# Ten DMA transposes in place of identity products for q and k of the fourth batch

## The chip, the cores and the metric

The kernel runs on one core of one Trainium2 chip. The metric is the device time of one execution in microseconds (us). Three runs of the kernel before are known, and one further execution was recorded by the hardware profiler; every view quoted below comes from that one.

A core has four engines that compute: TensorE (PE in the views; PEld is its weight load), VectorE (DVE), ScalarE (ACT) and GpSimd (POOL). SyncE (SP) only issues DMAs here. DMAs are issued by POOL and by SP, and are carried out by 16 DMA engines.

## The reference

There are B = 8 batches, H = 8 heads, S = 576 tokens, D = 64 elements per head, and 16 extra "beacon" keys and values per head. First comes attention, then a mixer over its output:

```python
scores = scale * q @ concat(beacon_k, k).T        # 576 x 592 per head, causal but for the beacons
a = softmax(scores)
x = a @ concat(beacon_v, v)                       # heads side by side: 576 x 512 per batch
h = x.T @ U @ V                                   # rank 32, along the tokens
u = x + h.T
out = u + relu(u @ w_ch1) @ w_ch2                 # 512 -> 2048 -> 512
```

Inputs and output are float32. The kernel computes in float16, with float32 sums.

## The kernel before

**Counting.** Batches are b = 0 to 7, so the fourth batch is b = 3. Two heads make a pair c = 0 to 3, and p = 4b + c counts all pairs.

**Loads and staging.** For the batches 0 to 3, q and k are loaded in float16 by `token_load` (L224) from POOL: partition p holds the six tokens 6p to 6p+5 of each head, so a descriptor reads 6 x 64 float32 in one piece (1536 bytes). `emit_loads` (L259) issues for one batch the beacon keys, two halves of k and two of q, and then v (`v_beacon`, and five `v_tokens`, L239). For the batches 4 to 7, `load_whole` (L844) loads q and k in "token order": tile j holds 128 consecutive tokens, one token per partition, so a descriptor reads 64 float32 (256 bytes). These loads go into a list `coming`, from which one is issued with each unit of the mixer that `fill` emits. Both forms go into staging tiles (`st0` for k and `st1` for q), of which there are two buffers each, in `qk_tiles`.

**Turning q and k.** The scores need q and k with the head elements on partitions (`qT`, `kT`). For the batches 0 to 3, `regroup` (L290, L292) copies a pair's columns together on DVE. Then `qkT_units` multiplies six pieces of 96 tokens by an identity on PE into one PSUM bank (`in_pair`, L297), and DVE copies the bank into `qT` or `kT` (L330; the beacons' 16 columns at L335). For the batches 4 to 7, `turns` (L861) makes ten DMA transposes on SP instead: k tile 0, the five tiles of q, then k tiles 1 to 4, each for all heads (L869). `kT` has two buffers, for even and odd batches, and `qT` two.

**Scores and values.** `visit` makes scores (L409) for one or more groups of a pair and lets ACT take their exponential (L418). Masks follow on DVE (L346, L348), and `av_unit` multiplies by v (L427) and divides by the sums on DVE (L435, L436) into `xb`.

**The mixer.** When a batch is done, `mix_units` runs. `turn` (L455) sends five DMA transposes `uT<-xb` from SP. `head` (L464) and `most` (L489) compute the rank 32 part on PE in four PSUM banks. `settle` (L476) adds these banks on DVE to what the transposes put into `uT`, and `end` (L502) does the last 80 tokens. The blocks of 512 rows of the mixer then run as units out of `queue`, one with each `fill(1)`. The blocks 0 and 1 are `mlp_units` (L751, L777, with DVE or ACT taking out each bank), the later ones `fast_units` (L607, L633). A block's input is turned back by DMA transposes `ut<-uT` (L745, L583) for the last sum, and results are stored from SP (L796, L658).

**What sets the order.** The whole stream is in `tc.manual_schedule`: each engine and each queue does its work in the order in which the program names it. The order around the change is written out by hand. The loop over p starts at p = 8. At p = 8 it calls `load_batch(3)`, and then plays the line `third[0]`; the pairs 8 to 11 are `third`, and from p = 12 (`P6`) on `long_slot` is used. The products that turn batch 3 stand as q12, k12, q13, k13 in `third`, and for the pairs 14 and 15 in `long_slot` at p = 12 and 13. First scores of batch 3 are `v11:23,12:0` in `third[3]`; the next are `v12:123`. At p = 12 the program names on SP, in this order: k tile 0 and q tiles 0 to 3 of batch 4 (`fill_turns(tr, NT)`), `uT<-xb` of batch 2 (`mix_between`), and the other five transposes of batch 4. `most` of batch 2 is in `long_slot` at p = 13.

**Limits on the queues.** POOL's DMAs use eight completion semaphores in turn, and so do SP's: a DMA waits until the one eight places before it on its own queue has landed.

**PSUM banks.** `pst` (L106) takes the bank that has been empty longest, in program order (`emptied.pop(0)`), and `emptying` puts a bank at the end of that list. A PE instruction that starts a bank waits for the engine that last read it.

Of the kernel before, what the change touches and what calls it, by code (L numbers as in the profile page):

```python
# [30 lines left out]
def kernel(  # L31
# [13 lines left out]
    nc = tc.nc  # L45
# [13 lines left out]
    nk = [min(P, SK - P * c) for c in range(NC)]  # L59

    q0 = [max(0, P * j - Nb) for j in range(NC)]
    nq = [min(S, P * (j + 1) - Nb) - q0[j] for j in range(NC)]
    NT = NC
# [113 lines left out]
    kTs = [const.tile([P, NH2, NC * P], F16, name=f"kT{i}", tag=f"kT{i}") for i in range(2)]  # L177
    vss = [const.tile([P, NC * H * E], F16, name=f"vs{i}", tag=f"vs{i}") for i in range(2)]
# [41 lines left out]
    def beacon_load(eng, src, dst, hs):  # L220
        eng.dma_start(out=dst[0:Nb], in_=src[hs].rearrange("h p d -> p h d"))

    def token_load(eng, src, dst, hs):
        eng.dma_start(out=dst[0:TP, hs, :], in_=src[hs].rearrange("h (p j) d -> p h (j d)", j=TJ))  # L224

    def key_beacons(eng, src, dst, hs):
        beacon_load(eng, src, dst[TP:TB, hs, (TJ - 1) * D : TJ * D], hs)
# [15 lines left out]
    def v_loads(src, bsrc, vs):  # L243
        v_beacon(bsrc, vs)
        v_tokens(src, vs, ALLH)
# [4 lines left out]
    ALLH = slice(0, H)  # L250
# [5 lines left out]
        whole = [x[:, 0 : NT * DM].rearrange("p (j h d) -> p j h d", h=H, d=D) for x in t]  # L256
        return st, whole

    def emit_loads(b, L, vs):  # L259
        key_beacons(nc.gpsimd, beacon_k[b], L[0][0], ALLH)  # L260
        for hs in HALVES:
            token_load(nc.gpsimd, k[b], L[0][0], hs)
            token_load(nc.gpsimd, q[b], L[0][1], hs)
        v_loads(v[b], beacon_v[b], vs)


    def keep_warm(ps, n, a=ident):
# [15 lines left out]
    def regroup(st, c, i, *copies, beacons=True):  # L283

        t = pairs.tile([P, TJ, 2, D], F16, name=f"pr{i}", tag=f"pr{i}")
        src = by_token(st[i][:, 2 * c : 2 * c + 2, :])
        w = TJ // len(copies)
        for a, copy in enumerate(copies):
            js = slice(w * a, w * (a + 1))
            copy(out=t[0:TP, js], in_=src[0:TP, js])  # L290
        if i == 0 and beacons:
            copies[0](out=t[TP:TB, TJ - 1], in_=src[TP:TB, TJ - 1])  # L292
        return t
# [539 lines left out]
    Ls, qTs, xbs = {}, {}, {}  # L833
    coming = []

    def load_batch(b):
        if b < DT0:
            Ls[b] = qk_tiles()
            emit_loads(b, Ls[b], vss[b % 2])
        else:  # L840
            coming.append(lambda: v_beacon(beacon_v[b], vss[b % 2]))
            coming.extend(lambda j=j: v_tokens(v[b], vss[b % 2], ALLH, [j]) for j in range(NT))
# [15 lines left out]
        while coming:  # L858
            coming.pop(0)()

    def turns(b):  # L861

        all_coming()
        new_qT(b)
        kn, qn = Ls[b][1]
        k_of = lambda j: (kn, kTs[b % 2], P * j, nk[j], j)
        q_of = lambda j: (qn, qTs[b], q0[j], nq[j], j)
        return [
            lambda n=n, dst=dst, o=o, m=m, j=j: nc.sync.dma_start_transpose(  # L869
                out=dst[:, :, ds(o, m)], in_=n[:m, j, :, :].rearrange("p h d -> p (h d)")  # L870
            )
            for n, dst, o, m, j in [k_of(0), *map(q_of, range(NT)), *map(k_of, range(1, NT))]
        ]

    HALVES = [slice(0, H // 2), slice(H // 2, H)]
# [19 lines left out]
    prs = {}  # L895
    V = nc.vector.tensor_copy

    def regroup_of(p):
        b, c = divmod(p, NH2)
        prs[p] = [regroup(Ls[b][0], c, i, nc.vector.tensor_copy) for i in range(2)]  # L900

    for i in range(2):
        nc.vector.memset(kTs[i][:, :, SK : NC * P], 0.0)
# [15 lines left out]
    def qkT_of(p):  # L919
        b, c = divmod(p, NH2)  # L920
        new_qT_of(p)
        copies = [(act_copy, nc.vector.tensor_copy) if p == 0 else (nc.vector.tensor_copy,)] * 2
        turns = by_heads(Ls[b][0], c)
        for i, t in enumerate(prs.get(p, ())):
            if t is not None:
                turns[i] = in_pair(prs[p])[i]
        return qkT_units(turns, qTs[b], kTs[b % 2], c, copies, Ls[0][0][0] if p == 0 else None)

    def expts_of(p):
        return [(lent if p in (2, 3) else expts)[(2 * p + i) % NE] for i in range(2)]  # L930
# [21 lines left out]
    ON_PE = (0, 1, 4)  # L952

    DT0 = 4
    LAG = 10
    HINT = 5
    FAST = 2
# [10 lines left out]
    def fill_turns(tr, n):  # L968
        for u in tr[:n]:
            u()  # L970
        del tr[:n]
# [64 lines left out]
    with tc.manual_schedule(engines={ENG.PE, ENG.Activation, ENG.DVE, ENG.SP, ENG.Pool}):  # L1036
# [182 lines left out]
        for p in range(NP1, NP):  # L1219
            b, c = divmod(p, NH2)  # L1220
            if c == (1 if b >= DT0 else 0) and b + 1 < B:
                load_batch(b + 1)
            if c == (1 if b + 1 == DT0 else 2) and DT0 <= b + 2 < B:
                load_whole(b + 2)
            qk = qkT_of(p + 2) if P6 <= p and p + 2 < min(NP, DT0 * NH2) else []
            if c == 0 and DT0 <= b + 1 < B and b != DT0:
                tr = turns(b + 1)
            if c == NH2 - 1 and b + 1 == DT0:
                tr = turns(b + 2)
            if c in (0, NH2 - 1) and b + 1 == DT0:  # L1230
                fill_turns(tr, NT)
            if p == P6:
                mix_between(b - 1)
            if c == 0 and b + 1 >= DT0:
                fill_turns(tr, 2 * NT)
            if p < P6:
                play(third[c])
            else:
                long_slot(p, c, av_of(p), qk or [lambda: None] * 2)
# [110 lines left out]
```

## Time and profile before

| | |
|---|---|
| three runs | 341.88, 343.14, 347.04 us (median 343.14) |
| the profiled execution | 340.93 us, of which the span from first to last instruction is 339.3 |
| granted TensorE clock | 1.00 |
| busy DVE, ACT, POOL (share of the span) | 69%, 53%, 40% |
| mean rate of the DMAs | 124 GB/s |

How to read the rows of the next part: in a timeline a row has start, length, engine, line, operation, out<-in, a count if several neighbours were put together, and in square brackets the idle time before it and what ended that. In a chain a row has start, length and what. "SPq" is SP's queue issuing a DMA. In DMA views, q0 is the queue that POOL feeds, and q1 the one that SP feeds; a queue's row has packets, MB, and the time that its packets took as a share of 16 engines' window. A row under "issues" ends with the median time from issue to landing.

### The profile page before, as it was taken

The page shows a single profiled execution, that of the slowest core. Times are in us where ns is not written, and L with a number is a line of the kernel's source. Part 1 is how long each engine was busy: PE and PEld are TensorE (multiplying, and loading weights), DVE is VectorE, ACT ScalarE, POOL GpSimd, SP SyncE. Part 2 cuts the span into 40 slices and gives each one's busy share as a digit, 9 for nine tenths or more (in the row PEclk, how much of TensorE's full clock was granted, in tenths as well). Part 3 has the DMA queues.
Part 4 walks back from the last instruction along what each step waited for, and adds up shares of the span by engine and source line. Part 5 has one row for each costly group of instructions (what it writes and reads, how often), then busy time and mean ns, then how long its engine had stood idle before and what let it go on. Part 6 is the DMA issues. An engine that isn't in the chain of part 4 may idle for free.

```text
span 339.3 us, 8838 instructions
## 1 busy us (share of the span) xinstructions
PE 329.8 (97%) x3494; PEld 212.0 (62%) x3494; DVE 234.1 (69%) x585; ACT 178.7 (53%) x383; POOL 136.1 (40%) x175
## 2 busy tenths in 40 slices
PE   8799999999999999999999999999999999999993
PEld 4465655455555456865688888755875675585493
DVE  6586885689989748765876677687776963743652
ACT  5957951478851677257734784468445403502500
POOL 8986724765140900677066805040130014013041
PEclk9999999999999999999999999999999999999999
DMA  8999999999997994999999999944213304104113
GB/s 159 141 175 138 183 196 194 200 192 139 138 118 152 153 141 86 101 169 157 151 112 155 187 143 104 132 140 87 66 64 93 73 31 126 31 33 124 31 37 99
DMA packets 150832, 41.97 MB, mean 124 GB/s; under 512 B 132096, under 2 KB 149696, under 8 KB 150784
## 3 DMA queue, kind: packets, MB, share of 16 engines
q0 software_dynamic: 87568, 18.18, 74.6%
q1 hardware_dynamic: 62992, 22.87, 37.4%
q8 instruction: 29, 0.48, 0.6%
q10 hardware_dynamic: 224, 0.30, 0.3%
q14 instruction: 19, 0.16, 0.2%
HBM read 37.45 MB, written 9.44 MB: 138 GB/s over the span
## 4 chain that ended last, share of the span: by engine, by line
PE 88%; DMA 4%; POOL 3%; DVE 1%; issue 1%; ACT 1%; POOLq 0%; DVEq 0%
PE gps L607 29%; PE po L427 9%; PE mpsD L633 7%; PE cps L777 7%; PE gps L751 7%; PE sps L409 5%; DMA vs<-in_v_dram 4%; PE mpsF L633 4%; PE mpsC L633 4%; PE mpsA L633 4%; PE mpsB L633 4%; PE mpsE L633 3%; POOL vs L239 1%; PE sps L370 1%; POOL st L224 1%
## 5 line engine op out<-in xcount | busy, mean ns | idle before, releaser
L418 ACT ACTIVATE expt<-sps 128x496 f16<-128x496 f32 (+2 forms) x192 | 82.0, 539 | 52.6 <-PE sps L409 52.6
L607 PE MATMUL gps<-uT,w 128*128 128x512 f16 (+1 forms) x512 | 103.7, 353 | 0.0
L654 POOL TENSOR_TENSOR ob<-ob,ut 128x512 f32<-128x512 f32 x26 | 30.8, 1188 | 139.9 <-DVE ob L654 127.7
L633 PEld LDWEIGHTS <-gT 128*128 128x128 f16 x800 | 75.1, 98 | 11.3 <-issue 2.1
L618 ACT ACTIVATE gT<-gps 128x512 f16<-128x512 f32 x84 | 49.7, 609 | 58.8 <-PE gps L607 54.3
L607 PEld LDWEIGHTS <-w 128*128 128x128 f16 x512 | 47.6, 98 | 41.4 <-issue 1.6
L239 POOL DMA_DIRECT2D vs<-in_v_dram x50 | 39.7, 804 | 15.3 <-DMA w<-in_moe_w_ch_dram 12.3
L596 DVE TENSOR_TENSOR gT<-gT 128x1024 f16<-128x1024 f16 (+2 forms) x77 | 39.5, 540 | 4.2 <-ACT gT L618 3.3
L427 PEld LDWEIGHTS <-expt 128*128 128x128 f16 x900 | 33.9, 98 | 10.9 <-issue 2.7
L427 PE MATMUL po<-vs,expt 128*128 128x65 f16 x900 | 36.5, 194 | 1.1 <-DMA vs<-in_v_dram 1.0
L616 DVE TENSOR_SCALAR gT<-gps 128x512 f16<-128x512 f32 x28 | 19.3, 691 | 24.0 <-PE gps L607 23.4
L436 DVE TENSOR_TENSOR xb<-po,rec 128x320 f16<-128x320 f32 x64 | 31.4, 491 | 2.2
L751 PE MATMUL gps<-uT,w 128*128 128x512 f16 x128 | 32.5, 379 | 0.1
L777 PE MATMUL cps<-w,gT 128*128 128x512 f16 x128 | 31.1, 379 | 0.0
L435 DVE RECIPROCAL rec<-po 128x5 f32<-128x5 f32 x64 | 12.1, 189 | 19.0 <-PE po L427 18.7
L346 DVE TENSOR_TENSOR expt<-expt,bigmask 128x512 f16<-128x512 f16 x54 | 22.5, 417 | 1.2 <-ACT expt L418 1.2
L409 PE MATMUL sps<-qT,kT 64*128 64x80 f16 (+4 forms) x288 | 22.6, 281 | 0.0
L376 ACT ACTIVATE expt<-sps 128x496 f16<-128x496 f32 (+2 forms) x48 | 20.4, 564 | 0.6 <-PE sps L370 0.6
L409 PEld LDWEIGHTS <-kT 64*128 64x128 f16 x288 | 10.2, 94 | 13.4 <-issue 9.3
L777 PEld LDWEIGHTS <-gT 128*128 128x128 f16 x128 | 11.2, 98 | 11.6 <-issue 1.3
L852 POOL DMA_DIRECT2D st<-in_q_dram x20 | 16.9, 874 | 3.2 <-DVE expt L348 1.4
L751 PEld LDWEIGHTS <-w 128*128 128x128 f16 x128 | 10.6, 97 | 10.8 <-issue 1.2
(125 smaller groups left out, 384.8 us busy)
## 6 DMA issues: line engine op xcount, KB each, us to landing
out_dram<-ob SPq DMA_DIRECT2D x55, 128.0 KB, 1.9
vs<-in_v_dram POOLq DMA_DIRECT2D x18, 128.0 KB, 7.9
w<-in_moe_w_ch_dram POOLq DMA_DIRECT2D x4, 512.0 KB, 6.4
w<-in_moe_w_ch_dram POOLq DMA_DIRECT2D x2, 1024.0 KB, 12.8
out_dram<-ob SPq DMA_DIRECT2D x8, 256.0 KB, 4.9
st<-in_k_dram POOLq DMA_DIRECT2D x12, 128.0 KB, 7.2
st<-in_q_dram POOLq DMA_DIRECT2D x12, 128.0 KB, 8.3
st<-in_k_dram POOLq DMA_DIRECT2D x4, 288.0 KB, 11.9
```

Of the source, the lines that this page charges most:

```text
L239: nc.gpsimd.dma_start(out=dst[a : a + nq[j], j, :, :], in_=src[hs, ds(q0[j], nq[j]), :].rearrange("h p d -> p h d"))
L409: nc.tensor.matmul(banks[i][:, ds(at0 + o, w)], kT[hp, c, ds(P * ch, P)], qT[hp, c, ds(qa, w)], start=True, stop=True, skip_group_check=le ...
L418: nc.scalar.activation(out=at[p][3][i][:, ds(SLOT * g, gw[g])], in_=bank[:, ds(at0, gw[g])], func=AF.Exp, scale=scale)
L427: nc.tensor.matmul(po[:, j, :], ex[0 : nk[c], ds(blk[(c, j)], P)], vs[0 : nk[c], ds(c * H * E + h * E, E)], start=(c == 0), stop=(c == j),)
L436: nc.vector.tensor_tensor(out=xb[:, :, ds(h * D, D)], in0=po[:, :, 0:D], in1=r.broadcast_to([P, NT, D]), op=ALU.mult)
L596: nc.vector.tensor_tensor(out=o[:, ds(d0, n)], in0=x[:, ds(d0, n)], in1=y[:, ds(d0, n)], op=op)
L607: nc.tensor.matmul(g[:, ds(o, w)], w1[:, cc, ts(dc, P)], uT[:, cc, ds(at, w)], start=(cc == 0 and o == 0), stop=(cc == NCC - 1), skip_grou ...
L618: nc.scalar.activation(out=cell["g"][:, dc, :], in_=g, func=AF.Relu)
L633: nc.tensor.matmul(ps, a()[:, d, ds(P * i, P)], bm[:, d, ds(c0, w)], start=fresh and d == 0 and (i == 0 or key != bank), stop=d == HF - 1, ...
L654: eng.tensor_tensor(out=out, in0=x, in1=y, op=ALU.add)
L751: nc.tensor.matmul(g[:, 0:n], w1[:, cc, ts(dc, P)], uT[:, cc, ds(r0, n)], start=(cc == 0), stop=(cc == NCC - 1))
L777: nc.tensor.matmul(ps[:m, :], gT["t"][:, dc, ds(P * i, m)], w2[:, dc, :], start=(dc == 0), stop=turned and dc == NDC - 1, skip_group_check ...
```

## The change

Batch 3 is loaded in token order by POOL like the batches 4 to 7, but at one place in `emit_loads`, not through `coming`: the beacon keys, k tile 0, the five tiles of q, k tiles 1 to 4, then v. Right after these loads, still at p = 8 and ahead of `third[0]`, SP is given the ten transposes of batch 3. The regroups of the pairs 12 to 15, their identity products and their copies are gone; their places in the hand-written order stay, empty.

```diff
-    def emit_loads(b, L, vs):
-        key_beacons(nc.gpsimd, beacon_k[b], L[0][0], ALLH)
+    def emit_loads(b, L, vs, whole=""):
+        if "k" not in whole:
+            key_beacons(nc.gpsimd, beacon_k[b], L[0][0], ALLH)
         for hs in HALVES:
-            token_load(nc.gpsimd, k[b], L[0][0], hs)
-            token_load(nc.gpsimd, q[b], L[0][1], hs)
+            for i, (name, src) in enumerate((("k", k[b]), ("q", q[b]))):
+                if name not in whole:
+                    token_load(nc.gpsimd, src, L[0][i], hs)
+        if whole:
+            for u in whole_loads(b, L, whole):
+                u()
         v_loads(v[b], beacon_v[b], vs)

+    def whole_loads(b, L, names):
+        def part(i, j):
+            src, m = ((k[b], nk), (q[b], nq))[i]
+            nc.gpsimd.dma_start(
+                out=L[1][i][m[j] - nq[j] : m[j], j, :, :],
+                in_=src[:, ds(q0[j], nq[j]), :].rearrange("h p d -> p h d"),
+            )
+        units = []
+        if "k" in names:
+            units += [lambda: beacon_load(nc.gpsimd, beacon_k[b], L[1][0][:, 0, :, :], ALLH)]
+        units += [lambda n=n, j=j: part("kq".index(n), j) for n, j in order_of(names)]
+        return units
+
+    def order_of(names):
+        return [x for x in [("k", 0)] + [("q", j) for j in range(NT)] + [("k", j) for j in range(1, NT)] if x[0] in names]
...
-            emit_loads(b, Ls[b], vss[b % 2])
+            emit_loads(b, Ls[b], vss[b % 2], AHEAD if b == DT0 - 1 else "")
...
-    def turns(b):
+    def turns(b, names="kq"):
...
-            for n, dst, o, m, j in [k_of(0), *map(q_of, range(NT)), *map(k_of, range(1, NT))]
+            for n, dst, o, m, j in [(k_of if x == "k" else q_of)(i) for x, i in order_of(names)]
...
-        prs[p] = [regroup(Ls[b][0], c, i, nc.vector.tensor_copy) for i in range(2)]
+        prs[p] = [
+            None if b == DT0 - 1 and name in AHEAD else regroup(Ls[b][0], c, i, nc.vector.tensor_copy)
+            for i, name in enumerate("kq")
+        ]
...
-        return qkT_units(turns, qTs[b], kTs[b % 2], c, copies, Ls[0][0][0] if p == 0 else None)
+        units = qkT_units(turns, qTs[b], kTs[b % 2], c, copies, Ls[0][0][0] if p == 0 else None)
+        return [
+            (lambda: None) if b == DT0 - 1 and name in AHEAD else u for name, u in zip("qk", units)
+        ]
...
     DT0 = 4
+    AHEAD = "kq"
...
                 load_batch(b + 1)
+                if b + 1 == DT0 - 1:
+                    fill_turns(turns(b + 1, AHEAD), 2 * NT)
```

## The prediction

> **What bounds the kernel now.** I read the page's first and fourth parts, PE's waits, and then the chain around the place of the change.
>
> ```profile
> span 339.3 us, 8838 instructions
> PE 329.8 (97%) x3494; PEld 212.0 (62%) x3494; DVE 234.1 (69%) x585; ACT 178.7 (53%) x383; POOL 136.1 (40%) x175
> PE 88%; DMA 4%; POOL 3%; DVE 1%; issue 1%; ACT 1%; POOLq 0%; DVEq 0%
> ```
>
> PE is busy 97% of the span and holds 88% of the chain. So only two things move the time: PE work that goes, and new waits of PE. The wait list around the change has one entry of some size:
>
> ```profile
> PE tps L297 <- DVE gT L766: 0.5, 1, 0.5
> ```
>
> The chain there, with the products that turn batch 3:
>
> ```profile
> 75.49 0.68 DVE pr L292
> ...
> 76.56 0.61 DVE gT L766
> ...
> 81.93 0.26 PE tps L297 x6
> ...
> 106.28 0.27 PE tps L297 x6
> ```
>
> The reader is to see that the first row belongs to the regroup of pair 12, that an eviction is queued behind it (second row), for which PE then waits 0.5 us, and that batch 3's eight groups of six products (first and last shown) take 0.26 to 0.27 us each of the chain.
>
> Now the DMAs, which PE does not wait for today. Two windows show them at work, the first with POOL's loads alone, the second with four transposes `ut<-uT` among them:
>
> ```profile
> q0 software_dynamic: 4669, 0.59, 246.8%
> ...
> q1 hardware_dynamic: 16, 0.00, 0.5%
> ```
>
> ```profile
> GB/s 150 138 176 182 218 225 294 301 208 163 149 161 259 172 163 172 114 54 29 42 47 19 9 82 158 159 157 164 169 166 160 168 146 156 158 188 154 149 152 158
> DMA packets 5651, 1.22 MB, mean 152 GB/s; under 512 B 5523, under 2 KB 5523, under 8 KB 5650
> q0 software_dynamic: 3392, 0.42, 131.5%
> q1 hardware_dynamic: 2258, 0.78, 76.2%
> ```
>
> The first is 84 to 88 us: 4669 small packets in 4.0 us, 1167 per us. The second is 74 to 82 us: in twice the time POOL's queue gets only 3392 packets through. Transposes are dear to the loads beside them; that decides the forecast.
>
> **The change part by part.**
>
> *PE.* Eight groups go: 8 x 0.265 = 2.1 us. The wait of 0.5 us goes with the regroup in front of it. PE's next work moves up, so the most that can be won is 2.6 us.
>
> *DVE.* Gone are eight copies out of PSUM (6.0 us, below) and the copies of four regroups. DVE is 69% busy and off the chain, so beyond the 0.5 us I count nothing; the cover is PE's own work.
>
> ```profile
> L330 DVE COPY qT<-tps 128x576 f16<-128x576 f16 x4 | 3.0, 749 | 0.0
> L330 DVE COPY kT<-tps 128x576 f16<-128x576 f16 x4 | 3.0, 748 | 0.0
> ```
>
> *POOL and its queue.* POOL's issues, and the time to landing of the first (58.64) and last (62.32) of batch 3's q and k loads and of the last of batch 4's (83.53):
>
> ```profile
> 58.64 0.53 POOL L221 DMA_DIRECT2D st<-in_beacon_k_dram  x1 [1.00 <-DVE pr L290]
> 62.32 0.67 POOL L224 DMA_DIRECT2D st<-in_q_dram  x1
> 71.33 0.53 POOL L221 DMA_DIRECT2D st<-in_beacon_k_dram  x1 [0.97 <-DVE expt L346]
> 83.53 0.74 POOL L852 DMA_DIRECT2D st<-in_q_dram  x1 [1.37 <-DMA st<-in_k_dram]
> 91.64 0.53 POOL L221 DMA_DIRECT2D vs<-in_beacon_v_dram  x1 [7.38 <-PE po L427]
> 109.62 0.54 POOL L221 DMA_DIRECT2D st<-in_beacon_k_dram  x1 [12.87 <-DMA kT<-st]
> ...
> st<-in_beacon_k_dram POOLq DMA_DIRECT2D x1, 16.0 KB, 6.3
> ...
> st<-in_q_dram POOLq DMA_DIRECT2D x1, 288.0 KB, 10.1
> ...
> st<-in_q_dram POOLq DMA_DIRECT2D x1, 80.0 KB, 6.3
> ```
>
> Batch 3's four loads land between 58.6 + 6.3 = 64.9 and 62.3 + 10.1 = 72.4: 7.5 us, with part of a store among them. Whole, they are 576 x 8 x 2 = 9216 packets, at 1167 per us 7.9 us. That is 0.4 us more, or 1.3 if the store's 0.9 us (256 KB at the 301 GB/s that the second window reaches) is taken out of the old figure. I take 0.9. Eleven issues instead of five cost POOL nothing that shows, as its DMAs land six to ten us after issue, queued behind each other. Behind them wait batch 3's v, then batch 4's k and q (71.33 to 83.53), then batch 4's v.
>
> *SP and the transposes.* Ten transposes of together 1168 token rows of 1 KB are 4672 packets of 256 bytes, 9.1 times the 512 of a full one. From the second window: 8.0 us, less 3392 / 1167 = 2.9 for the loads, less 0.9 for the store in it (the 128 packets of 512 B or more), leave 4.2 us for 2130 packets, four transposes: 1.0 us each. Bounds: 0.7, if the 1.2 us in which the rate row falls under 60 GB/s is no doing of theirs; 1.2, if the store cost nothing. The ten cost 9.1 us of the DMAs' time (6.6 to 11). I take 1.0: it is the row of the same stretch with the same neighbours.
>
> [...]
>
> *Who waits for that.* SP's queue:
>
> ```profile
> 70.43 6.09 SPq L745 DMA_TRANSPOSE ut<-uT  x4
> 85.42 1.19 SPq L869 DMA_TRANSPOSE kT<-st  x1
> 87.15 5.31 SPq L869 DMA_TRANSPOSE qT<-st  x4
> 92.55 7.64 SPq L455 DMA_TRANSPOSE uT<-xb  x5
> ...
> 97.63 1.27 SPq L455 DMA_TRANSPOSE uT<-xb  x1
> ...
> uT<-xb SPq DMA_TRANSPOSE x1, 5.5
> ```
>
> Ten issues of 1.3 us follow batch 3's loads on SP, from about 66 to 80. They are put ahead of the last store of block 0 and the four `ut<-uT` of 70.43; those slip to 80 to 86, and have time: block 1 takes its first sum only after its sixteen units of L751 and four of L777. What does not have time stands behind batch 4's first five transposes: `uT<-xb` of batch 2. Those five wait for batch 4's loads, which wait behind batch 3's in one queue. The fourth `uT<-xb` lands at 97.63 + 5.5 = 103.1 today. Its reader:
>
> ```profile
> 104.46 0.39 PE L489 MATMUL ups<-Vsb,qts 32*128 32x496 f16 x4
> 110.08 0.76 PE L409 MATMUL sps<-qT,kT 64*128 64x208 f16 x8
> ...
> 104.87 2.42 DVE L476 TENSOR_TENSOR uT<-ups,uT 128x496 f16<-128x496 f32 x4
> 108.43 0.75 DVE L330 COPY kT<-tps 128x576 f16<-128x576 f16 x1
> 109.17 0.48 DVE L476 TENSOR_TENSOR uT<-uend,uT 128x320 f16<-128x320 f32 x1
> 109.57 0.68 DVE L560 TENSOR_TENSOR wt<-w 128x1024 f16<-128x1024 f16 x1
> ```
>
> The settle (L476) starts at 104.87 because PE is done then; the transpose has 1.8 us to spare. In the changed kernel PE arrives 2.3 us earlier. Everything on DVE queues behind a late settle, and PE runs on only while there are banks. The scores at 110.08 take six: four are those of `ups`, the last, by the order of the list, that of `uend`, which L476 empties 109.57 - 104.87 = 4.7 us after the settle began, 4.0 without the kT copy (0.74) that goes. PE needs it 0.35 us before the scores' end, at 110.5 today. So with the fourth `uT<-xb` landing at T, PE is at today's place at T + 4.0: net = T - 106.5, but never under -2.6. Up to T = 103.9 the delay is free.
>
> *T.* 103.1 today, plus 0.9 for the loads, plus 9.1 for the transposes. Two unknowns of opposite sign: POOL had nothing to issue between 83.53 and 91.64, so its queue ran dry for some 2.8 us, which a backlog uses up (-2.8 to 0). And batch 5's loads, which today wait until 109.62 for batch 4's transposes to release their staging buffer, find batch 3's buffer free and follow batch 4's v at once, so up to four of them (0.9 us each, 1024 / 1167) get ahead (0 to +3.5). No row tells these apart; I let them cancel. T = 113.1.
>
> *Sum.* -2.6 + (113.1 - 103.9) = +6.6 us on the profiled execution: span 345.9, time 340.93 + 6.6 = 347.5. That execution is 2.2 us under the median of 343.14, so 349.7 on the scale of the runs.
>
> *Batch 3's own scores.* They start in the groups below, 2.1 us earlier in the new kernel.
>
> ```profile
> 85.03 0.69 PE L409 MATMUL sps<-qT,kT 64*128 64x336 f16 x10
> 88.91 0.67 PE L409 MATMUL sps<-qT,kT 64*128 64x464 f16 x10
> ```
>
> The first needs k tile 0 and q tiles 0 to 3, the second all ten. The tenth is issued at about 80 and, with the 8.6 us from issue to landing that the quoted `ut<-uT` took (median of the four), lands near 88.6, against 86.8 wanted: a wait of some 2 us. It delays PE, not T, so the late settle contains it and it adds nothing to the sum; alone it would cost 2 us.
>
> ```profile
> ut<-uT SPq DMA_TRANSPOSE x4, 8.6
> ```
>
> **The rivals.**
>
> *The other side: the transposes are as cheap as a load's packets.* Then 4672 / 1167 = 4.0 us, T = 103.1 + 0.9 + 4.0 - 2.8 = 105.2, net -1.3: 339.6 profiled, 341.8 on the runs' scale; with T under 103.9 the full -2.6 (340.5). It decides at T = 106.5, 3.4 us after today's landing. For it: the four `qT<-st` from 87.15 on, behind which POOL had no more loads, went out at SP's own pace, 5.31 / 4 = 1.3 us. Against it: the second window, where loads are under way, as they will be. [...]
>
> *Partly late.* Transposes at 0.7 us, the dry time used up, no load of batch 5 ahead: T = 103.1 + 0.9 + 6.6 - 2.8 = 107.8, net +1.3: 342.2 profiled, 344.4.
>
> *Later still.* Batch 5's four loads get ahead and nothing is regained, or batch 4's loads are given batch 3's staging buffer and wait for its transposes as batch 5's do today (12.87 us in the row at 109.62): T = 116.6, net +10.1: 351.0 profiled, 353.2. For it: POOL's queue is never short of work in the new order. Against it: batch 2's buffer is free from the regroup of pair 11 on, before batch 3's.
>
> That the change does not do what it says is no case: the products and copies are gone from the program.
>
> **How the numbers follow.** Two per cent, about what a measurement of this kernel tells from no change, is 6.9 us, reached at T = 113.4. Late settle, T from 110 to 115.5: 0.58, of which 0.30 above +6.9. Later still: 0.20, above. Partly late: 0.11, within. As cheap as loads: 0.08, within. Something unseen that gains over 6.9 us: 0.03, since what goes is worth 2.6. So slower 0.30 + 0.20 = 0.50, same 0.28 + 0.11 + 0.08 = 0.47, faster 0.03. The likeliest gives 349.7; its own range, 346.6 to 352.1. The range over the cases, 342.5 to 355.5, leaves out the cheap transposes and the unseen gain below (0.11), and T over 118.9 above (less than 0.1).
>
> **What would show it.** PE has no L297 between 81 and 107 us and no 0.5 us wait near 77. The q0 queue stays busy from 65 to past 105 without a pause. Batch 4's q lands near 99 to 100 instead of 83.53 + 6.3 = 89.8, `uT<-xb` is issued after 101, and PE waits several us before the scores that stand at 110.08 today, with DVE L476 waiting for `uT<-xb`. Batch 5's beacon keys are issued before 105 instead of at 109.62. I am wrong if the ten transposes leave the landings of batch 4's q within 4 us of today's, or if DVE's settle starts before 106.

## The result, and the profile after

The changed kernel takes 357.31 us (median of 5 runs, 353.64 to 359.36); the kernel before, run beside it, 347.04 us (5 runs, 341.88 to 349.74). The ratio is 1.042, with a 95% interval of 1.037 to 1.046; like every ratio below it sets only the fast runs of both kernels against each other, and so leaves out three of before's five (347.04 us and over) and one of the changed kernel's (359.36), each over 1.5% above the fastest run of its kernel. The forecast was 349.7, with a range from 342.5 to 355.5. The profiled execution of the changed kernel took 353.64 us, 12.7 more than the 340.93 of before, where the sum had come to 6.6 more. Line numbers after the diff are 24 higher: L409 is now L433 (scores), L476 L500 (settle), L455 L479 (`uT<-xb`), L777 L801, L607 L631, L869 L893.

The page of the changed kernel (span and engines, the granted clock in 40 slices, the chain):

```profile
span 351.7 us, 8742 instructions
...
PE 332.5 (95%) x3446; PEld 210.6 (60%) x3446; DVE 222.8 (63%) x561; ACT 178.7 (51%) x383; POOL 141.3 (40%) x181
...
PEclk9999999999998589999999999999999999999999
...
PE 83%; DMA 5%; SPq 4%; ACT 3%; DVE 2%; issue 1%; DVEq 0%
```

PE's busy time rose by 2.7 us although 48 matmuls fewer are done (the slow clock below makes others longer), and DMA and SP's queue hold 9% of the chain instead of 4%. The clock row has a dip at slices 13 to 15, some 105 to 132 us. PE's waits in the changed kernel (total, times, longest):

```profile
PE sps L433 <- DVE uT L500: 8.6, 3, 7.9
PE sps L433 <- DMA kT<-st: 2.3, 1, 2.3
```

The same place in PE's timeline, changed kernel first, then before:

```profile
106.28 2.76 PE L801 MATMUL cps<-w,gT 128*128 128x512 f16 x12
116.91 0.33 PE L433 MATMUL sps<-qT,kT 64*128 64x208 f16 x1 [7.87 <-DVE uT L500]
117.48 2.35 PE L433 MATMUL sps<-qT,kT 64*128 64x208 f16 x6 [0.25 <-DVE uT L500]
120.27 0.54 PE L433 MATMUL sps<-qT,kT 64*128 64x464 f16 x1 [0.43 <-DVE uT L500]
120.75 4.80 PE L801 MATMUL cps<-w,gT 128*128 128x512 f16 x12
125.39 1.03 PE L631 MATMUL gps<-uT,w 128*128 128x512 f16 x4
```

```profile
110.76 2.76 PE L777 MATMUL cps<-w,gT 128*128 128x512 f16 x12
113.36 1.03 PE L607 MATMUL gps<-uT,w 128*128 128x512 f16 x4
```

PE was 1.1 us ahead of before when it started the twelve matmuls of the first row (107.39 before). Then it stood for 7.9 us. The scores ended at 120.8, 10.0 us behind the 110.84 of before. The twelve matmuls after them took 4.80 us instead of 2.76: two more microseconds that no wait shows. Block 2 (the first L631, L607 in before) begins at 125.39 instead of 113.36, 12.0 us late, and from there to the end the two kernels run nearly alike (the spans differ by 12.4). So nearly all of the loss is made in this one place, and it has three parts: the wait of 7.9 us, the scores (3.9 us instead of 0.76, as they need the settle's banks one after the other) and a slow stretch, which reaches behind them. The windows of the changed kernel show the last (after the busy columns: granted clock, DMA share, GB/s):

```profile
105.00:110.00 5.00, 4.03 (x23) 1.80 (x21) 0.00 (x0) 0.00 (x0) 2.79 (x4) 1.00 1.84 140
110.00:117.00 7.00, 0.10 (x1) 0.09 (x1) 0.82 (x2) 0.00 (x0) 2.63 (x4) 0.59 1.76 134
117.00:121.00 4.00, 3.17 (x9) 0.47 (x9) 3.96 (x9) 2.65 (x8) 0.00 (x0) 0.50 1.70 154
121.00:125.40 4.40, 4.40 (x13) 1.57 (x12) 2.51 (x7) 0.41 (x1) 0.00 (x0) 0.56 1.64 241
```

While PE stands, its granted clock falls to 0.50. Read in windows of 0.1 us it falls at 111.2, 2.2 us after PE stopped, and is back at 124.9.

Back along the queues. What DVE waited for, in the changed kernel:

```profile
116.18 2.42 DVE L500 TENSOR_TENSOR uT<-ups,uT 128x496 f16<-128x496 f32 x4 [12.08 <-DMA uT<-xb]
```

SP's queue there, with the issue of the fourth `uT<-xb` and its time to landing:

```profile
90.27 1.40 SPq L893 DMA_TRANSPOSE kT<-st  x1
96.83 5.67 SPq L893 DMA_TRANSPOSE qT<-st  x4
102.59 7.59 SPq L479 DMA_TRANSPOSE uT<-xb  x5
...
107.53 1.32 SPq L479 DMA_TRANSPOSE uT<-xb  x1
```

```profile
uT<-xb SPq DMA_TRANSPOSE x1, 8.6
```

And POOL's issues from batch 3's first load on, with the time to landing of batch 4's last q load (issued at 91.15):

```profile
57.68 0.53 POOL L221 DMA_DIRECT2D st<-in_beacon_k_dram  x1 [0.99 <-DVE pr L314]
...
91.15 0.73 POOL L876 DMA_DIRECT2D st<-in_q_dram  x1 [1.43 <-DMA st<-in_k_dram]
...
101.50 0.53 POOL L221 DMA_DIRECT2D st<-in_beacon_k_dram  x1 [1.07 <-DMA st<-in_q_dram]
102.03 3.46 POOL L876 DMA_DIRECT2D st<-in_k_dram  x4
```

```profile
st<-in_q_dram POOLq DMA_DIRECT2D x1, 80.0 KB, 10.4
```

Batch 4's last q load lands at 91.15 + 10.4 = 101.5 instead of 89.8. The four q transposes in SP's row at 96.83 need the q loads just ahead of that last one, `uT<-xb` of batch 2 stands behind them, and its fourth lands at 107.53 + 8.6 = 116.1 instead of 103.1. Batch 5's loads go out from 101.5 on, instead of 109.62. The DMAs hardly rest: between 65 and 106 us of the changed kernel there is one slice of 1 us that is not full, against 83 to 95 of before (busy share of 40 slices):

```profile
DMA  9999999999999999999999399999999999999999
```

```profile
DMA  9999999999999999999922999607930399641899
```

### The profile page after: what moved, and what is told of

It reads as the page before. It is cut to its first block, busy times and chain, and to the rows that moved or that the text cites. A ratio compares the mean times of both kernels' runs of the same rounds, so it can differ in the third digit from the quotient of the medians.

```text
span 351.7 us, 8742 instructions
## 1 busy us (share of the span) xinstructions
PE 332.5 (95%) x3446; PEld 210.6 (60%) x3446; DVE 222.8 (63%) x561; ACT 178.7 (51%) x383; POOL 141.3 (40%) x181
## 3 DMA queue, kind: packets, MB, share of 16 engines
q1 hardware_dynamic: 67984, 24.07, 38.4%
## 4 chain that ended last, share of the span: by engine, by line
PE 83%; DMA 5%; SPq 4%; ACT 3%; DVE 2%; issue 1%; DVEq 0%
PE gps L631 28%; PE po L451 7%; PE cps L801 7%; PE mpsD L657 7%; PE sps L433 5%; PE gps L775 5%; PE mpsF L657 4%; PE mpsC L657 4%; PE mpsB L657 3%; PE mpsA L657 3%; PE mpsE L657 3%; SPq L893 3%; DMA kT<-st 3%; DMA uT<-xb 2%; ACT expt L400 2%; DVE uT L500 1%
## 5 line engine op out<-in xcount | busy, mean ns | idle before, releaser
L631 PE MATMUL gps<-uT,w 128*128 128x512 f16 (+1 forms) x512 | 103.7, 352 | 0.0
L631 PEld LDWEIGHTS <-w 128*128 128x128 f16 x512 | 47.6, 98 | 41.4 <-issue 1.6
L239 POOL DMA_DIRECT2D vs<-in_v_dram x50 | 39.7, 804 | 16.0 <-DMA w<-in_moe_w_ch_dram 12.1
L433 PE MATMUL sps<-qT,kT 64*128 64x80 f16 (+4 forms) x288 | 25.1, 285 | 11.0 <-DVE uT L500 8.6
L801 PE MATMUL cps<-w,gT 128*128 128x512 f16 x128 | 32.6, 398 | 0.0
L433 PEld LDWEIGHTS <-kT 64*128 64x128 f16 x288 | 10.4, 94 | 25.8 <-issue 18.1
L459 DVE RECIPROCAL rec<-po 128x5 f32<-128x5 f32 x64 | 12.1, 188 | 20.6 <-PE po L451 20.4
L500 DVE TENSOR_TENSOR uT<-ups,uT 128x496 f16<-128x496 f32 x24 | 14.4, 664 | 12.6 <-DMA uT<-xb 12.1
L801 PEld LDWEIGHTS <-gT 128*128 128x128 f16 x128 | 11.9, 102 | 14.8 <-issue 5.0
```

Source lines behind the costliest of these rows:

```text
L239: nc.gpsimd.dma_start(out=dst[a : a + nq[j], j, :, :], in_=src[hs, ds(q0[j], nq[j]), :].rearrange("h p d -> p h d"))
L433: nc.tensor.matmul(banks[i][:, ds(at0 + o, w)], kT[hp, c, ds(P * ch, P)], qT[hp, c, ds(qa, w)], start=True, stop=True, skip_group_check=le ...
L631: nc.tensor.matmul(g[:, ds(o, w)], w1[:, cc, ts(dc, P)], uT[:, cc, ds(at, w)], start=(cc == 0 and o == 0), stop=(cc == NCC - 1), skip_grou ...
L801: nc.tensor.matmul(ps[:m, :], gT["t"][:, dc, ds(P * i, m)], w2[:, dc, :], start=(dc == 0), stop=turned and dc == NDC - 1, skip_group_check ...
```

## The experiments

Theory A: the ten transposes delay batch 4's loads, these delay batch 4's transposes on SP, and batch 2's `uT<-xb` stands behind them, so that DVE's settle and PE wait. Rivals: the whole loads do it (L), or the DMAs are simply behind, in whatever order (Q). A place to read each run by is the start of the settle, which lies 0.1 us behind the fourth landing when the settle waits for it.

**e1_whole_pe: the loads alone.** No transposes of batch 3; PE turns each pair by five identity products straight from the token-order tiles.

```diff
-                if b + 1 == DT0 - 1:
-                    fill_turns(turns(b + 1, AHEAD), 2 * NT)
...
+            for j in range(NT):
+                nc.tensor.transpose(
+                    ps[:, ds(at[j], m[j])], Ls[b][1][i][: m[j], j, 2 * c : 2 * c + 2, :], ident[: m[j], : m[j]]
+                )
+            nc.vector.tensor_copy(out=dst[:, c, 0:n], in_=ps)
```

> The loads of batch 3 as in the changed kernel (whole, token order, eleven DMAs), but no transposes: PE turns each pair by five identity products straight from the token-order tiles, with no regroups. Theory A (the ten transposes delay everything behind them, the fourth uT<-xb of batch 2 lands at 116.1 instead of 103.1 and the settle waits for it): without the ten, the landing falls back to 103 to 105, PE has no wait of over 1 us before the scores that stand at 110 in the kernel before, the granted clock stays 1.00, and the time is that of before less 0 to 2 us (ratio 0.993 to 1.003). Rival L (the eleven loads of 256 byte pieces are what delays the queue): the landing stays over 110 and the time 2% or more above before.

The fourth `uT<-xb` landed at 104.8 and PE had no wait before the scores, as A has it. But the ratio was 1.020 (1.010 to 1.030) where 0.993 to 1.003 was forecast: a miss. The loss had another place, seen in the waits of e1, in SP's queue, in the time to landing of SP's last row, and in POOL's queue:

```profile
PE mpsE L657 <- DVE uT L500: 5.3, 1, 5.3
```

```profile
135.29 6.53 SPq L479 DMA_TRANSPOSE uT<-xb  x5
...
139.19 1.28 SPq L479 DMA_TRANSPOSE uT<-xb  x1
```

```profile
uT<-xb SPq DMA_TRANSPOSE x1, 8.1
```

```profile
138.08 4.24 POOL L239 DMA_DIRECT2D vs<-in_v_dram  x5
```

The same three views of before, the time to landing again that of the fourth:

```profile
131.19 7.03 SPq L455 DMA_TRANSPOSE uT<-xb  x5
```

```profile
uT<-xb SPq DMA_TRANSPOSE x1, 2.5
```

```profile
139.12 4.23 POOL L239 DMA_DIRECT2D vs<-in_v_dram  x5
```

This is the next settle, batch 3's. Its `uT<-xb` were issued 4.1 us later than before, and so fell among batch 5's v loads, which go out at 138 to 139 in both kernels. The fourth then took 8.1 us to land instead of 2.5. A slip of 4.1 us became one of 9, and the clock halved behind PE's wait here too (147.1 to 153.9). The loads alone had made that slip: batch 4's last q load landed 4.1 us later than before in e1 (93.9), and 2.8 later in e11 below (92.6), where I had counted 0.9.

**e2_dummy: the transposes alone.** The kernel before, with ten transposes of the same sizes into a buffer that nobody reads.

```diff
                 load_batch(b + 1)
+                if b + 1 == DT0 - 1:
+                    room = wt.rearrange("p i d c -> p (i d c)")
+                    for n, m in enumerate((TP, nq[0], P, P, P, nq[0], P, P, P, NL)):
+                        nc.sync.dma_start_transpose(
+                            out=room[:, ds(512 * n, 4 * m)].rearrange("p (c m) -> p c m", c=NCC),
...
```

> The kernel before, with ten transposes of the same sizes (1168 rows of 1 KB) added on SP after batch 3's loads, into a buffer that nobody reads; loads, products and copies stay. Theory A: the ten alone cost the DMAs 9 to 10 us, the fourth uT<-xb lands at 111 to 114 (batch 5's loads cannot go early here), PE waits 5 to 8 us before the scores at 110, and the clock falls after that wait: 6 to 10 us over before (ratio 1.017 to 1.03). Rival L (loads): at most 1 us over before. Rival 'cheap transposes' of the prediction: landing at 104 to 107, 0 to 1 us over before.

The ratio was 1.029 (1.017 to 1.041). The settle began at 113.73, PE waited 4.9 and then 1.5 us, and the clock fell. Landing, waits and ratio lie in the forecast of A. A holds; L and the cheap transposes fall. Batch 4's last q load landed at 103.3, 13.5 us later than before. The prediction's rival of cheap transposes had 4.0 for the ten, its estimate from the packet rate of the loads; beside loads this run does not bear it out.

**e3_uT_first: SP's order, at one place.** `uT<-xb` of batch 2 ahead of batch 4's first five transposes.

```diff
-            if c in (0, NH2 - 1) and b + 1 == DT0:
-                fill_turns(tr, NT)
             if p == P6:
                 mix_between(b - 1)
+            if c in (0, NH2 - 1) and b + 1 == DT0:
+                fill_turns(tr, NT)
```

> The changed kernel, with the five uT<-xb of batch 2 put on SP ahead of batch 4's first five transposes; the other engines are the same. Theory A with SP's order as the reason: the five are issued as soon as batch 2 is done (98 instead of 102.6), the fourth lands near 110 instead of 116, and the time falls by 5 to 8 us against the changed kernel (ratio to before 1.015 to 1.025). Rival Q (the DMAs themselves are behind, whatever SP's order): the fourth lands after 114 and the ratio stays at 1.035 to 1.045.

The fourth landed at 107.2, earlier than forecast, and PE waited only 0.6 us for this settle. The ratio was 1.042 (1.032 to 1.052) all the same, where 1.015 to 1.025 was forecast: the wait had moved to the next settle, as in e1, because batch 3's `uT<-xb` stands behind batch 5's transposes. PE's longest wait in e3:

```profile
PE mpsE L657 <- DVE uT L500: 7.0, 1, 7.0
```

So theory A was too narrow, and Q was still possible. Theory B replaced it: any due transpose that stands behind transposes and loads that are not yet due is late once the DMAs are full.

**e4_q_only: half of it.** `AHEAD = "q"`.

> The changed kernel with only q of batch 3 loaded whole and transposed; k is loaded, regrouped and turned by PE as before: five of the ten transposes. Theory A, a cost in proportion to the DMAs' work: the fourth uT<-xb lands at 108 to 110, PE waits 2 to 4 us, ratio 1.005 to 1.018. Rival (the cost comes from something that any one transpose of batch 3 brings, such as the freed staging buffer): the landing stays over 113 and the ratio over 1.03.

The settle began at 109.51 and the ratio was 1.017 (1.007 to 1.027): in proportion, as forecast. (1.9 us of PE's waits in its profile lie at batch 3's settle, as in e1.)

**e6_hold5: batch 5's loads later in the list.** `load_whole(5)` called at p = 15 instead of 13.

> The changed kernel, with batch 5's q and k loads put into the list two pairs later (p = 15 instead of 13), so that they cannot stand ahead of batch 2's uT<-xb. If these loads are the 3 us by which the landing (116.1) missed the forecast 113.1, the fourth uT<-xb lands at 112.5 to 113.5 and PE's wait before the scores shrinks from 8.6 to 5 to 6 us; rival: they cost nothing, the landing stays at 115.5 to 116.5. Batch 5's transposes then come later and stand ahead of batch 3's uT<-xb, as in e1 and e3, so a second late settle may eat the gain: ratio to before 1.03 to 1.045 in both cases, and the landing decides.

Ratio 1.040 (1.029 to 1.050), settle at 118.80. The edit did not do what I wanted: POOL's order was the same, and the loads went out at 102 anyway. It says nothing on what holding batch 5's loads brings; e14 does. But it shows the same thing a second time: with these loads beside it, the fourth `uT<-xb` took 8.3 us from issue (110.43) to landing.

**e7_uT_both: SP's order, at both places.** As e3, and batch 3's `uT<-xb` ahead of batch 5's first five transposes.

```diff
             if p == P6:
                 mix_between(b - 1)
+                fill_turns(tr, NT)
...
                 long_slot(p, c, av_of(p), qk or [lambda: None] * 2)
+            if c == NH2 - 1 and b + 1 == DT0:
+                fill_turns(tr, NT)
```

> The changed kernel, with uT<-xb put on SP ahead of the next-but-one batch's first five transposes at both places: batch 2's (p = 12, as in e3) and batch 3's (p = 15). Theory B (no lack of DMA time as such: the loss is that the due transposes stand in line behind transposes and loads that are not due): batch 3's uT<-xb is issued at 131 to 135 instead of 139.5, lands before batch 5's v loads start (140), the 7.0 us wait of e3 at mpsE goes, what is left is some 3 us before batch 3's own scores; ratio 1.00 to 1.012. Rival Q (DMAs are behind whatever the order; the wait only moves on): another wait of 5 us or more shows, ratio over 1.03.

Ratio 1.004 (0.998 to 1.010). Of the 14 us or so that the changed kernel lost, nearly all is back with ten DMA issues moved in one queue and nothing else changed. PE's waits in e7, the first for batch 3's own scores:

```profile
PE sps L433 <- DMA kT<-st: 3.4, 2, 1.8
...
PE sps L433 <- DVE uT L500: 0.6, 1, 0.6
```

B holds and Q falls, as no wait of 5 us shows: the DMAs had the time, the order on SP did not give it to the transposes that were due.

**e8_warm: the clock.** The changed kernel, with 90 matmuls that nobody reads where PE stands. A few operations of DVE, and a store, that the program names in the same unit are put behind them.

```diff
+                    for _ in range(90):
+                        nc.tensor.matmul(
+                            state["left"], ident, w1[:, 0, 0 : 512 - NCC * NL], start=True, stop=True,
...
```

> The changed kernel with the same order of everything, and 90 extra matmuls of 192 columns (into columns of the uend bank that nobody reads) that PE does while it waits for the settle. It adds work and no result. If the granted clock falls because PE stands still for 8 us, it stays at 1.00 here and the twelve L801 matmuls after the scores take 2.76 us as before instead of 4.80: 2 to 2.5 us less than the changed kernel, ratio 1.030 to 1.038. Rival (the clock falls for another reason, such as the load on the DMAs): they stay at 4.8 and the ratio at 1.04 or over.

PE's timeline in e8 (the mixer's lines lie 8 further on), and a window (granted clock after the busy columns):

```profile
113.73 7.59 PE L1251 MATMUL uend<-w,ident 128*128 128x192 f16 x90
121.78 0.25 PE L433 MATMUL sps<-qT,kT 64*128 64x208 f16 x1 [0.47 <-DVE uT L500]
...
125.43 2.76 PE L809 MATMUL cps<-w,gT 128*128 128x512 f16 x12
128.03 1.03 PE L639 MATMUL gps<-uT,w 128*128 128x512 f16 x4
```

```profile
113.70:121.70 8.00, 7.62 (x91) 7.45 (x90) 0.65 (x2) 0.00 (x0) 1.49 (x2) 1.00 1.83 141
```

Here the clock stayed at 1.00 and the twelve matmuls took 2.76 us, where the changed kernel had 0.50 and 4.80: the stand caused the fall of the clock. The time did not fall as forecast (1.043, 1.034 to 1.052), since the settle began at 121.06 in this execution, 4.9 us later than in the profile of the changed kernel. PE had been 4.85 us behind before the 90 matmuls (its twelve matmuls before them start at 111.13 instead of 106.28), so that they are not the reason. Batch 3's first load went out at 58.85 instead of 57.68, a slip that had grown to 5.3 us at the fourth `uT<-xb` (112.82); and PE waited 4.7 us in all for batch 3's `kT` (2.3 in the changed kernel), with the clock at half from 89.4 to 96.2. The table below takes the shift out.

**e14_hold5: batch 5's loads really held.** POOL first copies one element that batch 4's last transpose writes.

```diff
+                if b + 1 == DT0:
+                    coming.append(lambda: nc.gpsimd.tensor_copy(out=warm[0:1], in_=kTs[0][0:1, 0, SK - 1 : SK]))
                 load_whole(b + 2)
```

> The changed kernel, with batch 5's q and k loads really held: POOL first copies one element that batch 4's last transpose writes. (In e6 the place in the program moved, but POOL's own order was the same and the loads went out at 102 all the same.) If batch 5's loads are the 3 us by which the landing (116.1) missed 113.1, the fourth uT<-xb takes 5 to 6 us from issue to landing instead of 8.6, and PE stands still 3 us less there; if SP's own backlog of eight transposes in flight sets it, it still takes 8 to 9 us. Batch 5's transposes come late and stand ahead of batch 3's uT<-xb, so a second wait at mpsE is likely: ratio 1.03 to 1.05 either way.

Ratio 1.024 (1.014 to 1.035). POOL in e14, the fourth `uT<-xb` on SP, and its time to landing:

```profile
120.34 0.18 POOL L1258 COPY warm<-kT 1x1 f16<-1x1 f16 x1 [18.53 <-DMA kT<-st]
120.98 0.53 POOL L221 DMA_DIRECT2D st<-in_beacon_k_dram  x1 [0.46 <-issue]
```

```profile
109.18 2.18 SPq L479 DMA_TRANSPOSE uT<-xb  x1
```

```profile
uT<-xb SPq DMA_TRANSPOSE x1, 3.7
```

The fourth `uT<-xb` needed 3.7 us from issue to landing instead of 8.6, and landed at 112.9 instead of 116.1, though it was issued 1.6 us later. The rival, SP's own backlog, falls. As this execution was late from the start (batch 3's first load at 59.03), the 4.9 us from issue to landing are what batch 5's loads, let go early by the freed staging buffer, cost the transpose, and not the 3.2 us between the two landings. PE's wait before the scores fell from 7.9 to 2.9 us, and the second wait that I feared did not come.

**The table.** In the kernels in which PE waited over 2 us at batch 2's settle, or would have without the extra matmuls, the start of the settle and of block 2 (first L631, before L607) can be set against before, where the sum's rule "net = T - 106.5" means a settle start less 106.6:

| kernel | settle starts | by the rule | block 2 starts, less 113.36 | over the rule | the twelve matmuls |
|---|---|---|---|---|---|
| changed | 116.18 | +9.6 | +12.0 | 2.4 | 4.80 |
| e2 | 113.73 | +7.1 | +10.4 | 3.3 | 4.78 |
| e4 | 109.51 | +2.9 | +5.2 | 2.3 | 3.73 |
| e6 | 118.80 | +12.2 | +14.3 | 2.1 | 4.41 |
| e14 | 112.97 | +6.4 | +9.3 | 2.9 | 5.30 |
| e8, PE kept busy | 121.06 | +14.5 | +14.7 | 0.2 | 2.76 |

The rule held to 0.2 us where the clock stayed up; where it fell, 2 to 3 us came on top (1.6 and 2.6 in e4 and e2, which keep the kT copy of 0.7 us that the rule leaves out). It held as well in e3 and e7, in which PE waited only 0.6 us there and the clock stayed: by the rule +0.7 and +1.7, block 2 +0.9 and +1.9.

The slow stretches have a pattern. In windows of 0.1 us, the granted clock is at half for 3.4 us (e4 at 154.5, e14 at 89.2), 6.8 (e1 at 147.1, e4 at 110.1, e6 at 89.2, e8 at 89.4), 10.2 (e2 and e14 at 113.1, e3 at 149.8, e6 at 116.5) or 13.7 (the changed kernel): one, two, three and four times 3.41 us. In e6 the falls and returns, 89.19, 96.02, 116.48 and 126.72, lie two, six and three such steps apart. In these runs the length of a wait alone did not tell whether the clock falls: in e4 a wait of 2.7 us brought it down, in e3 one of 3.0 us (for `kT`, at 87) did not.

**e9, e10, e11, e12, e15, e16: what the change is worth when the order is mended.** All have both `uT<-xb` first, as e7. e9 has `AHEAD = "q"`; e10 is the kernel before with that order; e11 is e1 with it; e12 is e9 with batch 4's v loads held until batch 2's fourth `uT<-xb` has landed; e15 is e7 with batch 4's q and k held until batch 3's tenth transpose has landed; e16 is e15 with the v loads held as in e12. The holds are one-element copies on POOL, as in e14.

```diff
+                    coming.append(lambda: nc.gpsimd.tensor_copy(out=warm[0:1], in_=uT[0:1, 0, at : at + 1]))
...
+                    coming.append(lambda: nc.gpsimd.tensor_copy(out=warm[0:1], in_=kTs[1][0:1, 0, SK - 1 : SK]))
```

> Only q of batch 3 whole and transposed (as e4), with both uT<-xb first (as e7). Theory B: half of the transposes, so no wait of over 1 us at batch 3's scores and at both settles, PE has half of the products less (1.1 us): 0 to 1.5 us under before, ratio 0.994 to 1.003. Rival Q: a wait of 2 us or more somewhere, ratio 1.01 or over.

> The kernel before (token loads, regroups, identity products, no new transposes) with the two uT<-xb put ahead on SP as in e7. It tells what the order alone is worth. Theory B: before has no wait for either uT<-xb, so nothing to win: ratio 0.997 to 1.003. Rival: the order alone wins 1 us or more, and the gain of e9 would be the order's, not the transposes'.

> e1 (loads whole, five identity products a pair, no regroups, no new transposes) with both uT<-xb ahead on SP. Theory B: e1's 2% came from the wait of 5.3 us at mpsE, for batch 3's uT<-xb that stood behind batch 5's transposes; it goes, and so does the fall of the clock: 0 to 2 us under before, ratio 0.993 to 1.000. Rival (the whole loads cost PE time in another way): ratio over 1.01.

> e9, and POOL now waits with batch 4's v loads until the fourth uT<-xb of batch 2 has landed (one element of it is copied on POOL). Those loads were landing among the five uT<-xb (95.9 to 105.3). Theory B: the fourth lands at 100.5 to 103 instead of 105.0, the wait of 1.5 us before the scores goes, ratio 0.988 to 0.997, 1 to 1.5 us under e9. Rival: batch 4's v or batch 5's loads come too late and bring a wait of over 2 us of their own (ratio 1.00 or over).

> e7 (all ten transposes, both uT<-xb first on SP), and POOL holds batch 4's q and k loads until the tenth transpose of batch 3 has landed (one element of it is copied on POOL). If only the order was wrong: the ten land by 85 to 86, the wait of 3.4 us for kT goes, no wait of over 1 us takes its place, 338 to 340 us, ratio 0.985 to 0.995. If DMA time is lacking: batch 4's loads now land among the uT<-xb of batch 2 (issued at 91 to 97), whose fourth lands after 106, or batch 4's q and k come late for the scores at 117; a wait of 2 us or more, ratio 1.00 or over.

> e15, with batch 4's v loads also held until the fourth uT<-xb of batch 2 has landed, as in e12. If only the order was wrong, as e15 or 1 us less, ratio 0.985 to 0.995; if DMA time is lacking, a wait for batch 4's v, q or k between 115 and 130, ratio 1.00 or over.

| kernel | transposes of batch 3 | ratio to before (95%) | longest wait of PE from 70 us on |
|---|---|---|---|
| e10 | none | 0.9962 (0.9925 to 0.9999) | 0.2 |
| e11 | none, five products a pair | 0.9977 (0.9938 to 1.0016) | 0.2 |
| e9 | five | 0.9963 (0.9917 to 1.0008) | 1.5 |
| e12 | five | 0.9951 (0.9918 to 0.9985) | 0.2 |
| e7 | ten | 1.0040 (0.9977 to 1.0103) | 1.8, twice for kT |
| e15 | ten | 0.9972 (0.9919 to 1.0025) | 0.9 |
| e16 | ten | 0.9955 (0.9903 to 1.0008) | 1.5 |

e11 confirms that e1's 2% were the order's. e9's wait of 1.5 us is over the 1 us of its forecast. e12's fourth transpose landed at 100.7 and that wait went, as forecast; the 1 to 1.5 us of time did not go with it (medians 340.40 and 340.71). But e10, with nothing of the change in it, has the same ratio as the best of them, just under its forecast of 0.997 to 1.003. Nor is that 0.4% shown to come from the order: its profiled execution is 1.2 us ahead of before's already at 79.09 (80.30 in before), ahead of everything that the edit moves (from 85 us on), and 0.9 us ahead at the end. So none of the 0.4 to 0.5% is shown to be a gain of the transposes, and starts of executions scatter by as much (batch 3's first load went out at 57.68 to 59.03 us in the profiles above). e15 and e16 came out between their two forecasts. e16's profiled execution has the shortest span of all (337.3 us, e10's 338.4, before's 339.3), with one wait left:

```profile
PE sps L433 <- DMA kT<-st: 1.5, 1, 1.5
```

Whether the remaining 1 us or so of the 2.6 is there in the mean of many runs stays open; the intervals overlap.

## Why the direction was right and the size wrong

- **What bounds, and what PE wins.** Right. PE was 2.0 us ahead at 83.71 (85.68 before), and there is no product of batch 3 between 81 and 107 us. It lost 2.3 us at batch 3's own scores (forecast: some 2, contained in the later wait) and was still 1.1 ahead at 106.28. That the late settle contains this wait held too, but it has a price of its own: in the profiles of e6, e8 and e14 the clock halved behind it (from 89.2 or 89.4 on).
- **DVE counted at nothing.** Right; DVE waited 12.1 us for one transpose.
- **The loads, +0.9.** Too small: 2.8 and 4.1 us in e11 and e1, which have the loads alone. "Eleven issues instead of five cost POOL nothing that shows" did not hold: in e1, whose first load of batch 3 went out when it did in before (58.63), POOL issued batch 4's beacon keys at 74.01 instead of 71.33 and its last q load at 86.63 instead of 83.53.
- **The ten transposes, +9.1.** Between the two figures that the runs give, and not a constant: batch 4's last q load landed 7.7 us later in the changed kernel than in e1 (101.5 and 93.9), and 13.5 later in e2 than in before. Their packets are 4992 by the traces (67984 in q1 against 62992), not 4672.
- **The mechanism.** Right in each link: `uT<-xb` issued after 101 (102.6), the fourth at 97.63 + 0.9 + 9.1 = 107.6 by the sum and at 107.53 in the trace, PE at its old place some 4 us after T, batch 5's beacon keys before 105 (101.5). That 107.53 fits so well is luck in part. Batch 4's last q load landed at 101.5 where 99 to 100 was forecast, and POOL's first load of batch 3 had gone out at 57.68, 1.0 us earlier than in before. In e6, with that load at 58.63 and the same order on the queues, the fourth `uT<-xb` was issued at 110.43.
- **The step that failed: "No row tells these apart; I let them cancel. T = 113.1."** The fourth landed at 116.1. From issue to landing it took 8.6 us where the sum kept the 5.5 of before. e6 and e8, which have batch 5's loads beside it as well, agree (8.3 and 8.2); e14, e2 and e4, which do not, have 3.7, 3.9 and 3.2. So these loads cost 4.3 to 5.4 us there, above the +3.5 that I had as their upper end. The time without them is 1.6 to 2.3 us under the 5.5 of before, in which batch 4's v loads were still under way beside the fourth (between 97.5 and 97.8 only q0 moves packets): something was won back, but not as much. That e14's landing, 112.9, is near the forecast is chance: its transpose was issued 1.6 us late and took 1.8 less than 5.5. The rival "later still" (T = 116.6, +10.1, chance 0.20) was the case that came, by the first of its two reasons: batch 5's loads ahead.
- **What was in no term, and the second step that failed: the clock.** It cost 2.0 us in the twelve matmuls, 2.4 over the rule in the table. "PE is at today's place at T + 4.0" priced a wait of PE at its own length. In the trace the clock fell to half (0.50) at 111.2, 2.2 us after PE's stop at 109.0, and stayed there until 124.9, 8.0 us after PE had started again (116.91); in e4 a wait of 2.7 us was enough. The runs do not show what sets the step of 3.41 us.
- **The sum, mended:** T = 116.1 gives +9.6, the slow clock +2.4: 12.0, against 12.7 measured on the profiled execution. That execution was the fastest of the five, and the runs' scale of +2.2 was too small: 3.7 lie between it and the median. The other four runs left no trace. e6 and e8, whose queues are in the changed kernel's order, show what can be later: the settle began at 118.8 and 121.1, and the clock was at half for 6.8 us behind the wait for `kT`. The granted clock of those four runs is 0.972 to 0.974, as in e6 (0.973) and under the 0.979 of the profiled one, which fits this; it is not shown.
- **What I did not ask:** what is late after that. e1 and e3 show the next batch's settle at the same edge. The changed kernel meets it at 151.96 without a wait, its PE and with it batch 5's v loads being 12 us late by then.

## What to carry to other kernels

Work was moved here from a busy engine to DMAs that the profile showed as hidden, and that was paid for where the next due transfer stood in line behind transfers that were not yet due. Ask for each queue what is due first, and put that first, before anything is added. Ten issues moved on SP took the ratio from 1.042 to 1.004, and with the order mended no version of the change is told apart from the kernel before with the same order. When PE is the bound engine and will wait, price a slow clock behind the wait as well (1.6 to 2.9 us here, behind waits of 2.7 to 7.9 us at batch 2's settle), and do not let two unknowns cancel when one of them is freed by the change itself.

## What the runs showed of the hardware

- Transposes and loads that were under way together landed late together here: the fourth `uT<-xb` of a batch took 2.5 us from issue to landing with nothing else on the DMAs (before, at 135), 3.7 with only SP's own transposes beside it (e14), 8.1 to 10.1 beside a stream of loads (e1 at 139, e7 at 98). Batch 4's last q load took 6.3 us in before and 10.4 in the changed kernel, where 159 of the 455 packets between 91.0 and 91.5 us were those of SP's queue.
- Ten transposes of 4992 packets pushed a load behind them by 13.5 us (e2), about three times what as many packets of a load take at the 1167 per us of the prediction's first window (4.3 us). With no load beside them the transposes of e14 were not dear: between 109.3 and 110.9 us SP's queue moved 1056 packets, nearly all of them in the first 1.0 us.
- PE's granted clock fell from 1.00 to 0.50 while it waited for batch 2's settle (in the changed kernel 2.2 us into a wait of 7.9 us), and was still at half in the work behind: the twelve matmuls that take 2.76 us took 3.73 to 5.30 in the changed kernel, e2, e4, e6 and e14. In e3 it stayed up through a wait of 3.0 us. The slow stretches measured lasted 3.4, 6.8, 10.2 or 13.7 us, one to four times 3.41. 90 matmuls of no use kept the clock at 1.00 at the settle (e8).
